# Filling the gaps between dependent VectorE steps in a fused attention and MLP kernel

## The chip, the cores and the metric

The kernel runs on one core of one Trainium2 chip. A core has five engines that run side by side and wait for each other by semaphores: TensorE (PE, matmuls), VectorE (DVE), ScalarE (ACT), GpSimd (POOL) and SyncE (SP, here only a DMA queue). The metric is the device time of one execution in microseconds, the median of three runs. A profile is one execution, recorded instruction by instruction; its span is a little shorter than the time of the run.

## The reference, cut to what matters

Top-k attention over 8 batches, 8 heads, 576 tokens and a head size of 64, and then an MLP with a PReLU whose slope is a vector over the hidden units.

```python
scores = scale * np.matmul(q, k.transpose(0, 1, 3, 2))         # 576 x 576 for each head
kth = np.partition(scores, -top_k, axis=-1)[..., -top_k:-top_k + 1]   # top_k = 32
scores = np.where(scores >= kth, scores, -1000000000.0)
attn = softmax(scores)                                           # written out in the original
x = heads side by side of np.matmul(attn, v)                     # 4608 x 512
h = x @ w_in                                                     # 4608 x 2048
g = np.maximum(h, 0.0) + alpha * np.minimum(h, 0.0)
out = g @ w_out
```

All inputs and the output are fp32. The kernel splits the PReLU as alpha * h + (1 - alpha) * max(h, 0). So the output is x times a precomputed matrix `w_lin` plus max(h, 0) times a scaled `w_out`, and VectorE only has to take the maximum.

## The kernel before: the parts that matter

The work is cut into 144 pieces ("duos"): piece n is two groups of 128 query rows against 576 keys. The main loop is a software pipeline. Turn n of it, called slot n below, handles a different stage of several pieces at once. For one piece the stages are:

1. TensorE forms the scores (`ps_sc`, in PSUM, one buffer). ScalarE copies them to SBUF (`s_sb`).
2. VectorE looks for the 32nd largest score of each row. It takes the top 8 of each of six groups of 96 (MAX8, `up` and `small`), merges them (`bot`, `th`), negates (`neg`) and takes MAX8 again (`n8`). This gives a first threshold `p`.
3. ScalarE compares the row with that threshold (`sg`, a sign) and counts (`cs`). GpSimd multiplies scores and signs (`y`). VectorE takes MAX8 over `y` (two rows of 576), picks the right one by the count (`eq`, `pk`) and sums to the exact threshold `KT`.
4. ScalarE forms `r`, which is huge below the threshold; GpSimd subtracts it from the scores; ScalarE takes Exp (`w`).
5. A DMA transposes `w` to `wT`. TensorE multiplies by v (`xo`). Once in two slots VectorE normalises (`rz`, `x`), and DMA transposes `x` to `xT`.
6. MLP: TensorE forms `ph` = h, VectorE writes max(h, 0) to `gT`, TensorE adds up `pz`, ScalarE copies it out (`o_sb`), and SyncE's DMA stores it. While TensorE has nothing to do, `keep_warm` lets it multiply zeros (`rest`).

Inputs are transposed on TensorE (`tps`) and copied out of PSUM (`qkT`): for each pair of heads two copies of 512 columns and one of 128.

VectorE's part of a slot, with cuts:

```python
norm = on(n - 5) and n % 2 == 0 and n < ND + 4          # every second slot
if on(n):
    for i in range(2):
        for g in range(NG):                             # NG = 6
            m = DVE.max(out=(lo if g % 2 else up)[:, i, g // 2, :], in_=s[:, i, GW * g:GW * g + GW])
            ...
            if i == 0 and g == 1:
                kt_sum(n - 2)                           # KT <- pk
    DVE.tensor_tensor(bot, up, lo[:, :, :, ::-1], ALU.min)
    DVE.tensor_tensor(th[:, :, 0:24] ..., up, lo[:, :, :, ::-1], ALU.max)
    for i in range(2):
        DVE.max(out=th[:, i, 24:32], in_=bot[:, i, :, :])
    if norm:
        norm_a(n - 5)                                   # rz <- xo
else:
    ...
if on(n - 1):
    DVE.tensor_tensor(eq, io9 ..., cs ..., ALU.is_equal)
if on(n):
    DVE.tensor_scalar(neg, th, -1.0, None, ALU.mult)
if on(n - 1):
    DVE.max(out=p9[:, 0, 1:9], in_=y[:, 0, :])          # 576 columns
if norm and on(n):
    norm_b(n - 5)                                       # x <- xo, rz
h_dve()                                                 # gT <- ph
if on(n):
    for i in range(2):
        DVE.max(out=n8[:, i, :], in_=neg[:, i, 0:31])
if on(n - 1):
    DVE.max(out=p9[:, 1, 1:9], in_=y[:, 1, :])
if on(n):
    DVE.tensor_scalar(p9n[:, :, 0:1], n8[:, :, 7:8], -1.0, None, ALU.mult)
...
if on(n - 1):
    DVE.scalar_tensor_tensor(out=pk, in0=eq, scalar=BIG, in1=p9, ...)
```

In slots without normalisation the compiled kernel has `eq` ahead of `bot`, as the instruction list shows.

The main loop, with cuts:

```python
for n in range(ND + 4):                                 # ND = 144
    end = n >= ND
    if not h_pe() and not end:                          # ph, at most one group
        keep_warm()
    ... st_av(m)                                        # xo of piece n - 5
    st_count(n - 1); st_y(n - 1)                        # sg, cs; y
    st_exit(n + 1)                                      # s_sb <- ps_sc
    did = o_pe()                                        # one part of pz, if its PSUM bank is free
    dve_slot(n, late)
    st_relu(n - 2, 0); st_relu(n - 2, 1)                # r; GpSimd's subtraction
    run(n, "prep", ...)                                 # tps
    st_qk(n + 2)                                        # ps_sc
    ... if not (end or ready() > 2) or not o_pe():      # a second part of pz
            if not end and not did:
                keep_warm()
    st_exp(n - 3)                                       # w, wT
    busy = False
    while pend:                                         # copies out of PSUM (qkT)
        tail = n >= 4 and tuple(pend[0][0].shape[2:]) == (64,)
        prep_evac(DVE.tensor_copy if tail else ACT.copy)
        busy = busy or not tail
    run(n, "scale")                                     # w_out scaled: ScalarE and VectorE, 512 columns each
    if end or not busy:
        o_act()                                         # o_sb <- pz
    ...
```

`o_pe` starts no new part while a finished `pz` has not been copied out. After slot 147 a short loop works off what is left of the MLP.

Of the kernel before, what the change touches and what calls it, by code (L numbers as in the profile page):

```python
# [8 lines left out]
FP32 = mybir.dt.float32  # L9
# [8 lines left out]
NG = 6  # L18
# [17 lines left out]
def fast_path(tc, q, k, v, moe_w_in, moe_w_out, moe_alpha, out, flag):  # L36
# [27 lines left out]
    with ExitStack() as ctx:  # L64
# [169 lines left out]
        def dve_slot(n, f_late):  # L234
# [7 lines left out]
            norm = on(n - 5) and n % 2 == 0 and n < ND + 4  # L242
            if on(n):
                s = T["s", n]
                up = two.tile([128, 2, NG // 2, 8], FP32, name="up", tag="up")
                for i in range(2):
                    for g in range(NG):
# [5 lines left out]
                        if i == 0 and g == 1:  # L253
                            kt_sum(n - 2)

# [4 lines left out]
                                     lo[:, :, :, ::-1], ALU.max), [(0, 48)], [(48, 72), (80, 104)])  # L260
                for i in range(2):
                    o = 48 + 32 * i
                    sm(DVE.max(out=th[:, i, 24:32], in_=bot[:, i, :, :]), [f"bot{n % 2}"], [(o + 24, o + 32)])
                if norm:
                    norm_a(n - 5)
            else:
                kt_sum(n - 2)
# [3 lines left out]
            if on(n - 1):  # L271
                y, p9, cs = T.pop(("y", n - 1)), T.pop(("p9", n - 1)), T.pop(("cs", n - 1))
                sm(DVE.tensor_tensor(eq, io9.unsqueeze(1).to_broadcast([128, 2, 9]),
                                     cs.unsqueeze(2).to_broadcast([128, 2, 9]), ALU.is_equal),
                   [(146, 155)], [(128, 146)])
            if on(n):
                neg = two.tile([128, 2, 32], FP32, name="neg", tag="neg")
                sm(DVE.tensor_scalar(neg, th, -1.0, None, ALU.mult), [(48, 112)], [f"neg{n % 2}"])
            if on(n - 1):
                DVE.max(out=p9[:, 0, 1:9], in_=y[:, 0, :])  # L280
            if norm and on(n):
                norm_b(n - 5)
            h_dve()
            if on(n):
                for i in range(2):
                    o = 112 + 8 * i
                    sm(DVE.max(out=n8[:, i, :], in_=neg[:, i, 0:31]), [f"neg{n % 2}"], [(o, o + 8)])
            if on(n - 1):
                DVE.max(out=p9[:, 1, 1:9], in_=y[:, 1, :])
            if on(n):  # L290
                p9n = three.tile([128, 2, 9], FP32, name="p9", tag="p9", bufs=4)
                sm(DVE.tensor_scalar(p9n[:, :, 0:1], n8[:, :, 7:8], -1.0, None, ALU.mult), [(112, 128)], [f"p9{n % 4}"])
# [683 lines left out]
```

The softmax here doesn't subtract the row's maximum and nothing guards it: scores larger than these inputs give would overflow.

## Time and profile before

| what | value |
|---|---|
| time, median of 3 runs | 846.79 us (846.05 to 848.18) |
| span of the profiled execution | 847.1 us |
| TensorE: busy, matmuls recorded | 771.6 us (91%), 5454 |
| granted TensorE clock, mean | 0.976 |
| `y` and the subtraction on GpSimd, 288 each | 362.8 and 363.0 us |
| MAX8 over `y`, 288 on VectorE | 215.3 us, 748 ns each |
| MAX8 over 96 columns, 1728 on VectorE | 428.9 us, 246 to 251 ns each |
| `gT`, 144 on VectorE | 97.6 us, 678 ns each |
| `qkT` of 512 columns, 63 on ScalarE | 35.8 us, 573 ns each |
| `o_sb`, 36 on ScalarE | 20.7 us, 576 ns each |
| `rest` (zeros), 296 matmuls on TensorE | 79.8 us, 400 ns each |

How to read it: an instruction's duration runs from its start to the moment its result is written. The next instruction of the same engine may start before that, so the durations of VectorE add up to more than its busy time, which counts each moment once. What a step costs its engine is the distance from its start to the start of the next one. A row of the timeline gives the start, the duration, the engine, the source line, the operation, what is written from what is read, the shape, and how many instructions are merged in it; a bracket at the end holds the idle time before it and who ended it. Nearly all instructions carry line 31, that of a recording helper, so they are told apart by the names of their tiles.

### The profile page before, as it was taken

Reading aid. Unit: us, or ns where it says so; the run is one execution under the profiler, and the core shown is the slowest. Engines: PE = TensorE matmul, PEld = TensorE weight load, DVE = VectorE, ACT = ScalarE, POOL = GpSimd, SP = SyncE. Lnnn points to the kernel's source line nnn. Section 1 sums busy time; section 2 is a strip of 40 time slices with the busy share of each in tenths; the row PEclk is TensorE's granted clock in tenths of the full one; section 3 lists DMA queues with packets and bytes.
Section 4 is the critical chain, followed back from the end, with each engine's and each line's share of the span. In section 5 each row is a group of like instructions: output and inputs, shape, how many; then the busy total and the mean of one; then the engine's idle time right before and its main releaser. Section 6 shows DMA issues by size and latency. Waiting matters only on the chain.

```text
span 847.1 us, 18646 instructions
## 1 busy us (share of the span) xinstructions
PE 771.6 (91%) x5454; PEld 436.0 (51%) x5454; DVE 784.2 (93%) x3947; ACT 779.3 (92%) x1285; POOL 757.0 (89%) x706
## 2 busy tenths in 40 slices
PE   8778899998999999989999999989989999999886
PEld 5334455555545555555455555555555555555553
DVE  4989999999999999999999999999999999999941
ACT  5999999999999999999999999998999999999840
POOL 3998999999999999999999999998999998999930
PEclk9889999999999999999999999998999999999989
DMA  6899865576657656656466668565565674544441
GB/s 129 187 210 190 163 122 106 89 125 121 124 104 125 124 109 113 126 116 129 102 116 120 119 118 132 110 129 116 91 132 108 119 132 85 95 82 91 84 99 42
DMA packets 344462, 100.29 MB, mean 118 GB/s; under 512 B 338192, under 2 KB 338208, under 8 KB 344352
## 3 DMA queue, kind: packets, MB, share of 16 engines
q1 hardware_dynamic: 341456, 92.42, 58.4%
q0 software_dynamic: 1696, 6.30, 3.1%
q8 instruction: 45, 0.74, 0.4%
q14 instruction: 65, 0.53, 0.2%
q10 hardware_dynamic: 1200, 0.30, 0.2%
HBM read 36.71 MB, written 9.44 MB: 54 GB/s over the span
## 4 chain that ended last, share of the span: by engine, by line
DVE 61%; PE 19%; ACT 14%; issue 2%; DMA 2%; POOL 2%; ACTq 0%; SPq 0%
DVE small L31 17%; DVE p L31 16%; DVE up L31 10%; DVE gT L31 7%; PE pz L31 5%; PE ps_sc L31 5%; ACT sg L31 4%; PE ph L31 4%; ACT s_sb L31 3%; ACT r L31 3%; PE xo L31 3%; DVE neg L31 2%; DVE bot L31 2%; DVE x L31 2%; ACT w L31 2%
## 5 line engine op out<-in xcount | busy, mean ns | idle before, releaser
L31 POOL TENSOR_TENSOR y<-s_sb,sg 128x576 f32<-128x576 f32 x288 | 362.8, 1281 | 55.2 <-ACT sg L31 53.3
L31 POOL TENSOR_TENSOR s_sb<-s_sb,r 128x576 f32<-128x576 f32 x288 | 363.0, 1283 | 0.4 <-ACT r L31 0.2
L31 ACT ACTIVATE sg<-s_sb,p 128x576 bf16<-128x576 f32 x288 | 221.5, 773 | 24.4 <-DVE p L31 23.0
L31 PE MATMUL ps_sc<-qkT 64*128 64x512 f32 (+2 forms) x768 | 184.3, 575 | 45.9 <-ACT s_sb L31 44.9
L31 DVE MAX8 p<-y 128x8 f32<-128x576 f32 x288 | 215.3, 748 | 4.9 <-POOL y L31 4.7
L31 DVE MAX8 up<-s_sb 128x8 f32<-128x96 f32 x864 | 212.3, 246 | 5.3 <-ACT s_sb L31 5.3
L31 DVE MAX8 small<-s_sb 128x8 f32<-128x96 f32 x864 | 216.6, 251 | 0.0
L31 ACT ACTIVATE r<-s_sb,KT 128x576 bf16<-128x576 f32 x288 | 208.5, 776 | 0.8 <-DVE KT L31 0.8
L31 ACT ACTIVATE w<-s_sb 128x1152 bf16<-128x1152 f32 x144 | 166.9, 1159 | 1.0 <-POOL s_sb L31 1.0
L31 ACT COPY s_sb<-ps_sc 128x1152 f32<-128x1152 f32 x144 | 159.1, 1105 | 4.0 <-PE ps_sc L31 4.0
L31 PE MATMUL ph<-xT,w_in_b 128*128 128x256 bf16 (+1 forms) x1408 | 151.4, 255 | 6.1 <-DVE gT L31 3.2
L31 PE MATMUL pz<-w_out_b,gT 128*128 128x512 bf16 x576 | 149.4, 382 | 0.0
L31 PEld LDWEIGHTS <-w_in_b 128*128 128x128 bf16 x1408 | 119.0, 99 | 47.0 <-issue 12.9
L31 PE MATMUL xo<-v,wT 128*128 128x65 bf16 (+3 forms) x1600 | 126.5, 198 | 8.1 <-DMA wT<-w 8.1
L31 PEld LDWEIGHTS <-wT 128*128 128x128 bf16 (+3 forms) x1600 | 97.4, 99 | 42.8 <-DMA wT<-w 10.9
L31 DVE TENSOR_SCALAR gT<-ph 128x512 bf16<-128x512 f32 x144 | 97.6, 678 | 14.8 <-PE ph L31 14.8
L31 PEld LDWEIGHTS ps_sc<-qkT 64*128 64x128 f32 (+1 forms) x768 | 54.0, 170 | 97.6 <-ACT s_sb L31 67.2
L31 PEld LDWEIGHTS ps_sc<-kd,qkT 128*128 128x128 f32 x256 | 39.3, 193 | 100.7 <-issue 99.9
L31 PEld LDWEIGHTS <-gT 128*128 128x128 bf16 x576 | 56.8, 99 | 54.5 <-issue 2.4
L31 PE MATMUL rest<-idle 128*128 128x512 bf16 x296 | 79.8, 400 | 2.9 <-ACT qkT L31 2.1
L31 PE MATMUL ps_sc<-kd,qkT 128*128 128x128 f32 x256 | 64.3, 334 | 0.0
L31 PE MATMUL pz<-w_lin_b,xT 128*128 128x512 bf16 x144 | 56.0, 389 | 0.7 <-ACT o_sb L31 0.7
(56 smaller groups left out, 671.0 us busy)
## 6 DMA issues: line engine op xcount, KB each, us to landing
k_st<-in_k_dram SPq DMA_DIRECT2D x64, 128.0 KB, 2.7
v_st<-in_v_dram SPq DMA_DIRECT2D x64, 128.0 KB, 2.8
out_dram<-o_sb SPq DMA_DIRECT2D x32, 256.0 KB, 2.4
q_st<-in_q_dram SPq DMA_DIRECT2D x62, 128.0 KB, 2.7
w_st<-in_moe_w_out_dram POOLq DMA_DIRECT2D x4, 1024.0 KB, 6.8
wT<-w SPq DMA_TRANSPOSE x144, 3.5
w_in_b<-in_moe_w_in_dram POOLq DMA_DIRECT2D x4, 512.0 KB, 7.2
k_st<-in_k_dram SPq DMA_DIRECT2D x32, 32.0 KB, 2.5
```

What stands on the lines that cost most here:

```text
L31: return self.tc.keep_in_program_order(f(*a, **kw))
```

## The change

It moves steps; no arithmetic is altered. Between two VectorE steps of which the second reads what the first wrote, it places one that depends on neither. In slots without normalisation `kt_sum` follows the last MAX8 over the scores, and the first MAX8 over `y` comes between the MAX8s over `bot` and `neg`. In slots with normalisation the reciprocal comes before `bot`, and the normalisation follows `th`. In the last slots `h_dve` comes first. ScalarE's copy of a finished `pz` goes ahead of Exp, and it is asked for more often. On TensorE `xo` goes ahead of `ph`. Up to slot 16 the 512-column copies of the input transposes go to VectorE and the 128-column ones to ScalarE, later the short ones to VectorE as before; the scalings of `w_out` are spread differently over slots 3 to 14.

```diff
+            def eq_():
+                cs = T.pop(("cs", n - 1))
+                sm(DVE.tensor_tensor(eq, ... ALU.is_equal), ...)
+            def row(i):
+                DVE.max(out=T["p9", n - 1][:, i, 1:9], in_=T["y", n - 1][:, i, :])
             if on(n):
 ...
-                        if i == 0 and g == 1:
+                        if i == (norm == 0) and g == (1 if norm else NG - 1):
                             kt_sum(n - 2)
+                if norm:
+                    norm_a(n - 5)
                 bot = ...
                 sm(DVE.tensor_tensor(bot, up, lo[:, :, :, ::-1], ALU.min), ...)
                 sm(DVE.tensor_tensor(th[:, :, 0:24] ..., ALU.max), ...)
+                if norm:
+                    norm_b(n - 5)
+                elif on(n - 1):
+                    eq_()
                 for i in range(2):
                     sm(DVE.max(out=th[:, i, 24:32], in_=bot[:, i, :, :]), ...)
-                if norm:
-                    norm_a(n - 5)
+                if norm and on(n - 1):
+                    eq_()
+                elif on(n - 1):
+                    row(0)
+                sm(DVE.tensor_scalar(neg, th, -1.0, None, ALU.mult), ...)
+                if norm and on(n - 1):
+                    row(0)
+                h_dve()
+                for i in range(2):
+                    sm(DVE.max(out=n8[:, i, :], in_=neg[:, i, 0:31]), ...)
+                if on(n - 1):
+                    row(1)
+                sm(DVE.tensor_scalar(p9n[:, :, 0:1], n8[:, :, 7:8], -1.0, None, ALU.mult), ...)
             else:
+                h_dve()
                 kt_sum(n - 2)
 ...                                    # the old order of these steps is taken out
         for f in range(NFT):
-            at(3 + f // 2 if f < 8 else f - 1, "scale", lambda f=f: scale_out(f))
+            at((3, 3, 4, 4, 5, 6, 7, 7, 8, 9, 10, 11, 11, 12, 13, 14)[f], "scale", lambda f=f: scale_out(f))
 ...
+            for m in [n - 5, n - 4] if n == ND + 3 else [n - 5]:
+                if on(m):
+                    st_av(m)
             if not h_pe() and not end:
                 keep_warm()
-            for m in [n - 5] if n < ND + 3 else [n - 5, n - 4] if n == ND + 3 else []:
-                if on(m):
-                    st_av(m)
 ...
             if on(n + 2):
                 st_qk(n + 2)
+            if end or ready() > 4 or all(len(d.shape) == 3 for d, _ in pend):
+                o_act()
 ...
-            busy = False
             while pend:
-                tail = n >= 4 and tuple(pend[0][0].shape[2:]) == (64,)
-                prep_evac(DVE.tensor_copy if tail else ACT.copy)
-                busy = busy or not tail
+                short = len(pend[0][0].shape) == 3
+                on_dve = short and n > 16 or pend[0][0].shape[1] == 512 and n < 17
+                prep_evac(DVE.tensor_copy if on_dve else ACT.copy)
 ...
-            if end or not busy:
-                o_act()
```

In the instruction lists of the two kernels the slots without normalisation now read: last MAX8, `KT`, `eq`, `bot`, `th`, two MAX8 over `bot`, MAX8 over `y`, `neg`, `gT`. Those with normalisation read: last MAX8, `rz`, `bot`, `th`, `x`, two MAX8 over `bot`, `eq`, `neg`, MAX8 over `y`, `gT`.

## The prediction

> **What bounds the kernel now.** I read the page first (busy shares, then the chain of work that ended last), next the busy times by window, then VectorE's timeline over two slots, the waits, and TensorE's timeline at the end.
>
> ```profile
> PE 771.6 (91%) x5454; PEld 436.0 (51%) x5454; DVE 784.2 (93%) x3947; ACT 779.3 (92%) x1285; POOL 757.0 (89%) x706
> ...
> DVE 61%; PE 19%; ACT 14%; issue 2%; DMA 2%; POOL 2%; ACTq 0%; SPq 0%
> ```
> Three engines lie within four per cent of each other, but the chain runs through VectorE for 61% of the span: VectorE binds, narrowly.
>
> ```profile
> 400.00:500.00 100.00, 93.62 (x689) 53.36 (x686) 98.83 (x509) 97.88 (x163) 96.05 (x87) 0.98 0.62 116
> ...
> 800.00:820.00 20.00, 15.85 (x161) 11.04 (x160) 11.58 (x39) 11.71 (x20) 12.57 (x11) 0.83 0.56 104
> 820.00:847.00 27.00, 19.98 (x173) 11.85 (x170) 5.45 (x11) 2.13 (x4) 0.00 (x0) 0.94 0.16 47
> ```
> The columns are PE, PEld, DVE, ACT, POOL, then the granted clock. In the middle VectorE is at 98.8% and ScalarE at 97.9%; in the last 47 us only TensorE has much to do, and at 800 to 820 its clock is down to 0.83.
>
> ```profile
> 405.94 0.14 DVE L31 TENSOR_SCALAR p<-small 128x2 f32<-128x2 f32 x1
> ...
> 406.32 0.25 DVE L31 MAX8 small<-s_sb 128x8 f32<-128x96 f32 x1
> 406.48 0.15 DVE L31 TENSOR_REDUCE KT<-pk 128x2 f32<-128x18 f32 x1
> 406.55 0.25 DVE L31 MAX8 up<-s_sb 128x8 f32<-128x96 f32 x1
> ...
> 408.51 0.28 DVE L31 MAX8 small<-bot 128x8 f32<-128x24 f32 x2
> 408.82 0.22 DVE L31 TENSOR_SCALAR neg<-small 128x64 f32<-128x64 f32 x1
> ...
> 411.07 0.14 DVE L31 TENSOR_SCALAR p<-small 128x2 f32<-128x2 f32 x1
> ...
> 416.55 0.14 DVE L31 TENSOR_SCALAR p<-small 128x2 f32<-128x2 f32 x1
> ```
> The two-element p closes each slot, so an odd slot takes 411.07 - 405.94 = 5.13 us and an even one (with the normalisation) 5.48. These two values come back through the whole middle; an even slot with a 128-column qkT copy in it takes 5.70. Durations overlap, so the cost of a step is the distance to the next start: a 0.25 us MAX8 costs 0.16, KT costs 0.07. But neg, which reads what the MAX8 pair wrote, starts 0.31 after it; an independent step starts 0.19 after it. That 0.12 is waiting that the busy share hides.
>
> ```profile
> ACT sg L31 <- DVE p L31: 23.0, 43, 2.2
> DVE gT L31 <- PE ph L31: 14.8, 8, 7.8
> DVE rz L31 <- PE xo L31: 14.4, 13, 2.6
> ```
> ScalarE waits for VectorE's p, little (23 us over 144 slots): it is the next limit. VectorE waits for xo 13 times.
>
> ```profile
> 808.21 1.89 PE L31 MATMUL ph<-xT,w_in_b 128*128 128x128 bf16 x16 [3.20 <-DVE gT L31]
> ```
> At the end TensorE stands 3.2 us for a gT that VectorE has queued behind steps still waiting for their inputs; the 16 matmuls after it take 1.89 us, where the same group takes 1.07 just before.
>
> **What the Trainium skill says.** "VectorE: DVE Perf Modes", The DRAIN you can't avoid, says that a Vector step has a flush behind it and that a step which is not held starts earlier. The trace agrees: 0.16 between independent MAX8s, 0.28 from the last of them to the dependent bot. The same page, Why PSUM operands drop a tier, caps an fp32 source in PSUM at the slowest mode; the trace has 0.69 us on VectorE for the 512-column qkT copy and 0.57 on ScalarE, so moving these copies buys ScalarE time with more of VectorE's. "TensorE: Matmul & The Clock Gate", HAM oscillation, warns that idle gaps bring the clock down. Here it happens after shorter gaps than the page's 3.4 us: after 1.92 us idle at 571.09, the four ps_sc matmuls take 2.08 instead of 1.13. "Perfetto Trace Analysis", Identifying the Most-Contended Engine, takes occupancy as a fair measure for Vector; here part of it is the 0.12 waits.
>
> **The change part by part.**
>
> Odd slots on VectorE. KT moves behind the last MAX8, into the 0.28 before bot. KT (0.16 after that MAX8), eq (+0.07) and bot (+0.07) make 0.30 where the trace has 0.29, so KT's 0.07 elsewhere is freed and 0.01 paid. A 576-column p goes between the bot MAX8s and neg, which frees the 0.12. Sum 0.18: 5.14 becomes 4.96.
>
> Even slots. The reciprocal (0.08) moves into the 0.28 before bot: free. But between the bot MAX8s and neg only eq is left, so neg waits 0.19 + 0.12 instead of 0.19 + 0.08 + 0.06. Gain 0.02: 5.48 becomes 5.46. Moving x (0.32) only changes its place.
>
> Four slots of the middle on VectorE (two odd, two even, one 128-column copy of 0.20 to 0.22): 5.14 + 5.70 + 5.14 + 5.48 = 21.46 before, 4.96 + 5.68 + 4.96 + 5.46 = 21.06 after, 1.9% less.
>
> ScalarE over the same four: sg, sg, s_sb copy, two r and w start 0.77, 0.76, 1.00, 1.34 and 1.05 us apart, 4.92 in all, and each 512-column copy (qkT or o_sb) adds 0.47. Three in four slots: 4 x 4.92 + 3 x 0.47 = 21.09. The change moves o_sb ahead of Exp but removes nothing here, so ScalarE stops VectorE's gain at about 21.1: the two become level. GpSimd's y starts are 5.29, 5.39, 5.23 and 4.94 apart when it doesn't wait, 20.85: just below. Three engines level within one per cent do not interlock without loss; I take 5.30 us a slot instead of 21.06 / 4 = 5.27.
>
> Slots 24 to 123 take 543.0 us now (150.8 to 693.8): 5.43 each, of which 536.5 is 25 x 21.46 and the rest xo waits and slots with two gT. After: 5.30, plus 0.02 for waits of that kind, is 532. Gain 11.
>
> Waits for xo. Attention's matmuls now come before h. An h group takes 0.87 us to the next start, but the reciprocal asks 0.56 earlier (0.16 after the last MAX8 instead of 0.28 + 0.12 + 0.12 + 0.19 = 0.71, rounded in the trace), so the margin grows by only 0.3. The x20 slots, with waits of 0.7, keep about half. Twenty groups of idle matmuls disappear (160 instructions fewer on TensorE, eight to a group) because o_pe finds its PSUM bank free more often. I count about 17 slots in which nothing fills TensorE between xo, h and the next scores, against six before: more gaps of 1.7 to 1.9 us, more slow-clock stretches. With h out of the way most cost some 0.2 us, so I set the net to zero.
>
> First 17 slots (to 111.6 us). ScalarE is at 29.8 of 30 us from 30 to 60. Ten 512-column copies leave it (4.7 us) and three short ones come (0.6); VectorE takes ten of 0.60 (6.0). Slots 3 to 16 on ScalarE: 14 x 4.92 + 16 scalings of 0.62 + small copies = 80; VectorE comes to 78; today's 84.7 contains a stop, near 60 us, in which xo and tps waited on loads and which cost ScalarE 2.6 us; the change does not touch it. 84.7 - 82.6 is 2.1, and 0.4 more from the copies in slots 0 to 2: gain 2.5. Slots 17 to 23: 1.
>
> Slots 124 to 143: ScalarE has few copies left, so VectorE's 0.10 a slot comes through: 2, and 0.5 from xo.
>
> The end. gT first removes the 3.2 us stop and most of the slow stretch (808 to 813: ph 0.8, xo 0.3, pz 1.0 over their usual times, about 2.1). Two output parts fewer remain behind slot 144 (14 instead of 16, at 1.08 each): 2.2. Sum 7.5. Against it, KT comes one gT (0.6) later and so do the last Exp and its transposes; those end before TensorE reaches them. I take 6.
>
> Sum: 11 + 0 + 2.5 + 1 + 2.5 + 6 = 23. From 846.8 this gives 824. Each term assumes that nothing new waits; I leave 2 us for that and predict 826.
>
> **The rivals.** (1) ScalarE becomes the bound earlier than I say, or GpSimd does. For: 97.9% and 96.1% busy. Then the middle stays at 5.36 to 5.40 a slot, the gain there is 3 to 7 and the time is 830 to 838. (2) TensorE's clock falls more often, as idle matmuls are gone. For: the gap at 571 cost VectorE 1.87 us; against: in only three of about six such gaps before did xo come late. If each of 17 gaps costs 1 us, the time is 838 to 842. (3) o_sb ahead of Exp waits on pz and stops ScalarE. Usually the part is done 1.4 us before; after a slow stretch not. A wait of 0.5 us in ten slots is 5 us: 831. (4) ScalarE absorbs more than I think because its short slots fall well, and the end gains the full 7.5: 819.
>
> **Range and chances.** Two per cent is 829.9. My 826 lies 4 us below that, while rivals 1 and 3 cross it. Range 817 to 837. Faster by over 2%: 0.68; within 2%: 0.29; slower: 0.03, as nothing in the change adds work to the binding engine after slot 17.
>
> **What would show it.** Odd slots of 4.96 and even slots of 5.46 where VectorE leads; an average near 5.3; ScalarE's wait for p well below 23 us in the middle, VectorE's waits for y and cs (ScalarE's counts) above; DVE no busier than before. No 3.2 us stop at the end, and less than 38 us from the last p to the end of the span, against 42.8 now. Wrong if odd slots stay above 5.1, if PEclk falls below 0.95, or if ScalarE shows waits for pz in the middle.

## The result and the profile after

The changed kernel takes 838.23 us (median of 4 runs, 837.63 to 838.66) where the kernel before takes 846.59 (4 runs on the same chip, 846.05 to 848.18). The ratio is 0.9898, 95% interval 0.9881 to 0.9915: 1% faster. The prediction was 826, or 2.4% faster. The two profiled spans are 847.1 and 836.9 us, 10.2 apart; the prediction's terms added up to 23. I cut both spans at VectorE's two-element `p`, which closes a slot:

| stage | before | after | gain | predicted |
|---|---|---|---|---|
| to the end of slot 16 | 111.57 | 110.58 | 1.0 | 2.5 |
| slots 17 to 23 | 39.20 | 38.26 | 0.9 | 1 |
| slots 24 to 123 | 543.04 | 538.54 | 4.5 | 11 |
| slots 124 to 143 | 110.50 | 107.63 | 2.9 | 2.5 |
| from the last `p` to the end of the span | 42.79 | 41.89 | 0.9 | 6 |

Two terms fell, the middle and the end; the early one came to less than half. First the page of the changed kernel, busy shares and the engines' shares of the chain of work that ended last:

```profile
PE 744.9 (89%) x5289; PEld 425.0 (51%) x5374; DVE 780.2 (93%) x3954; ACT 774.5 (93%) x1278; POOL 755.2 (90%) x706
...
DVE 49%; PE 23%; ACT 15%; DMA 6%; issue 3%; POOL 1%; SPq 1%; ACTq 0%
```

VectorE's share of the chain falls from 61% to 49%, while TensorE and DMA rise to 23% and 6%. VectorE has stopped leading in parts of the span, and other engines' waits have come in. Next, busy times by window of the changed kernel (length, then PE, PEld, DVE, ACT, POOL, granted clock, DMA share, GB/s):

```profile
400.00:500.00 100.00, 90.36 (x665) 52.21 (x677) 98.05 (x504) 97.96 (x162) 96.22 (x89) 1.00 0.61 120
...
812.00:837.00 25.00, 16.18 (x150) 10.29 (x152) 5.45 (x11) 1.76 (x3) 0.00 (x0) 0.90 0.13 41
```

In the middle VectorE (98.05%) and ScalarE (97.96%) are level, as predicted. At the end TensorE is busy for 16.18 of 25 us: the end still contains stops. VectorE's timeline of the changed kernel over an even and an odd slot:

```profile
406.43 0.14 DVE L31 TENSOR_SCALAR p<-small 128x2 f32<-128x2 f32 x1
...
408.48 0.25 DVE L31 MAX8 small<-s_sb 128x8 f32<-128x96 f32 x1
408.64 0.16 DVE L31 RECIPROCAL rz<-xo 128x4 f32<-128x4 f32 x1
408.76 0.20 DVE L31 TENSOR_TENSOR bot<-up,small 128x48 f32<-128x48 f32 x1
...
411.88 0.14 DVE L31 TENSOR_SCALAR p<-small 128x2 f32<-128x2 f32 x1
...
414.40 0.28 DVE L31 MAX8 small<-bot 128x8 f32<-128x24 f32 x2
414.64 0.76 DVE L31 MAX8 p<-y 128x8 f32<-128x576 f32 x1
415.32 0.21 DVE L31 TENSOR_SCALAR neg<-small 128x64 f32<-128x64 f32 x1
...
416.90 0.14 DVE L31 TENSOR_SCALAR p<-small 128x2 f32<-128x2 f32 x1
```

The even slot takes 411.88 - 406.43 = 5.45 us (predicted 5.46), the odd one 416.90 - 411.88 = 5.02 (predicted 4.96; 4.93 to 4.94 occurs too). The fillers do what they are for: `rz` sits inside the 0.28 us between the last MAX8 and `bot`, and the row of `y` has removed the wait ahead of `neg`. Yet slots 24 to 123 take 5.39 us on average. The time goes at the places where something waits, so to the waits of the changed kernel (us in total, times, longest):

```profile
PE xo L31 <- DMA wT<-w: 22.7, 18, 5.8
ACT o_sb L31 <- PE pz L31: 22.0, 6, 7.6
...
ACT sg L31 <- DVE p L31: 12.1, 24, 1.2
```

ScalarE's wait for `p` has halved from 23.0, as a faster VectorE should make it. The line to notice is `xo` waiting for `wT`: 22.7 us, against 8.1 before. And in slots 24 to 123 ScalarE's `o_sb` waits for `pz` three times (1.9 us), where it never did before. That was one of the things named as showing the prediction wrong.

### The profile page after: what moved, and what is told of

Read it like the earlier page. It is cut to its first block, busy times and chain, and to the rows that moved or that the text cites. A ratio compares the mean times of both kernels' runs of the same rounds, so it can differ in the third digit from the quotient of the medians.

```text
span 836.9 us, 18387 instructions
## 1 busy us (share of the span) xinstructions
PE 744.9 (89%) x5289; PEld 425.0 (51%) x5374; DVE 780.2 (93%) x3954; ACT 774.5 (93%) x1278; POOL 755.2 (90%) x706
## 4 chain that ended last, share of the span: by engine, by line
DVE 49%; PE 23%; ACT 15%; DMA 6%; issue 3%; POOL 1%; SPq 1%; ACTq 0%
DVE small L31 15%; DVE p L31 13%; DVE up L31 8%; PE ps_sc L31 7%; PE pz L31 6%; DVE gT L31 6%; DMA wT<-w 4%; ACT sg L31 4%; PE xo L31 4%; ACT r L31 4%; PE ph L31 4%; ACT s_sb L31 3%; ACT w L31 2%; DVE x L31 1%; DVE neg L31 1%
## 5 line engine op out<-in xcount | busy, mean ns | idle before, releaser
L31 PE MATMUL xo<-v,wT 128*128 128x65 bf16 (+3 forms) x1600 | 127.3, 199 | 24.4 <-DMA wT<-w 22.7
L31 PE MATMUL pz<-w_out_b,gT 128*128 128x512 bf16 x554 | 144.5, 382 | 3.5 <-DVE pk L31 0.2
L31 PEld LDWEIGHTS <-w_in_b 128*128 128x128 bf16 x1408 | 109.0, 98 | 15.5 <-issue 0.2
L31 PE MATMUL rest<-idle 128*128 128x512 bf16 x198 | 57.9, 401 | 2.5 <-DVE qkT L31 0.9
L31 ACT ACTIVATION_READ_ACCUMULATOR sg<-s_sb,p 128x1 f32 x288 | 55.7, 193 | 0.0
```

Source lines behind the costliest of these rows:

```text
L31: return self.tc.keep_in_program_order(f(*a, **kw))
```

## The experiments

Each ratio is to the kernel before on the same chip, with its 95% interval. Executions of one kernel can differ by up to 9.1 us (849.12 to 858.23 in the first case below), so a stage value, which comes from one profile, is relied on only where several kernels agree or the difference is far larger.

**VectorE's order alone.** All else as before: `h_pe` ahead of `st_av`, `o_act` behind Exp, old copies, old last slots. Against the changed kernel:

```diff
+            if not h_pe() and not end:
+                keep_warm()
             for m in [n - 5, n - 4] if n == ND + 3 else [n - 5]:
                 if on(m):
                     st_av(m)
-            if not h_pe() and not end:
-                keep_warm()
 ...   # o_act, copies and last slots: as undone one by one below
```

> VectorE's new order alone; output copies, first transposes, order of xo and h and the last slots as before. Theory A (the freed VectorE time is real, but the reciprocal now asks for xo 0.56 us earlier while TensorE still does h first): undisturbed odd slots near 5.0 us and even ones at 5.46, VectorE's waits for xo up from 14.4 us to 22 or more, time 839 to 843. Theory B (the order frees nothing, ScalarE takes it; the 8 us of the change come from its other parts): four slots stay at 21.4, time 845 to 847.

Measured: 854.11 us, 1.0085 (1.0045 to 1.0124). The reordering that gives the change its point is a loss by itself. The profiled execution is the quickest of the six; its span, 847.3, is that of the kernel before (847.1), so it does not show where the slower ones lose. Their times follow the granted clock: 849.12 to 851.83 us at 0.982 to 0.985, 856.39 to 858.23 us at 0.972 to 0.975. What the profile shows is that nothing is gained: odd slots take 4.94, and the middle still takes 544.46 us. From its waits:

```profile
DVE rz L31 <- PE xo L31: 29.6, 35, 2.6
```

`rz` waited for `xo` 14.4 us in the kernel before and waits 29.6 here; in slots 24 to 123 alone it is 22 waits and 14.1 us instead of 5 and 4.5. One of them, from the timelines of VectorE and TensorE of this kernel:

```profile
402.47 0.18 DVE L31 RECIPROCAL rz<-xo 128x4 f32<-128x4 f32 x1 [0.52 <-PE xo L31]
```
```profile
400.79 1.03 PE L31 MATMUL ph<-xT,w_in_b 128*128 128x256 bf16 x8
401.66 0.78 PE L31 MATMUL xo<-v,wT 128*128 128x65 bf16 x10
```

The h group starts at 400.79 and holds `xo` back by 0.87, until 401.66; the reciprocal, now asked for earlier, stops for 0.52. What the fillers freed on VectorE is spent waiting for `xo`.

**Attention ahead of h alone**, in the kernel before:

```diff
+            for m in [n - 5] if n < ND + 3 else [n - 5, n - 4] if n == ND + 3 else []:
+                if on(m):
+                    st_av(m)
             if not h_pe() and not end:
                 keep_warm()
-            for m in ... (the same three lines)
```

> The kernel before, with only xo moved ahead of h on TensorE. Theory A (order of VectorE and order of TensorE are worth something only together): waits for xo in the middle (4.5 us) go, odd and even slots stay at 5.14 and 5.48: 841 to 844. Theory B (xo first is the gain by itself, VectorE's order nothing): 835 to 838.

Measured: 838.53 us, 0.9884 (0.9857 to 0.991). One moved loop gives as much as the whole change. The middle takes 540.2 us, with odd slots still at 5.14 and no wait of `rz` for `xo` in it. Stage by stage it is 3.4, 0.8, 2.8, 1.5 and 1.8 us shorter than the kernel before, so most of the gain lies outside the middle. Over the whole span:

```profile
PE xo L31 <- DMA wT<-w: 14.9, 13, 2.3
...
DVE rz L31 <- PE xo L31: 5.1, 4, 2.6
```

The waits for `wT` show up here already: they come with attention's place at the head of TensorE's slot.

**The whole change without it.** In the changed kernel only the two blocks of the first diff are exchanged.

> The changed kernel with h ahead of xo on TensorE again. Theory A (xo first is what makes the earlier reciprocal affordable): waits for xo rise from 11.9 to 20 us or more, time 842 to 846. Theory B (xo first does harm, as TensorE now stands for wT with h behind it: waits for wT were 10.9 us before and 31.3 after on the weight loads): waits for wT back near 11 us, gT waits for ph down from 19.3, time 834 to 837.

Measured: 848.10 us, 1.0014 (0.9997 to 1.0031). Without attention ahead of h the other four parts together give nothing; the middle even takes 546.3 us, with 14.4 us of waits of `rz` for `xo`. The fillers give VectorE time that only an earlier `xo` lets it use; how much that is then worth is shown further down.

**The output copy behind Exp again.** In the changed kernel:

```diff
-            if end or ready() > 4 or all(len(d.shape) == 3 for d, _ in pend):
-                o_act()
 ...
+            busy = False
             while pend:
 ...
+                busy = busy or not short
 ...
+            if end or not busy:
+                o_act()
```

> The changed kernel with the output copies behind Exp and only in slots without a 512-column copy, as before. Theory A (freeing the bank of pz earlier packs two output parts into slots in which TensorE is already full, which costs the 8 us of late slots in the middle): slots 51, 52, 87, 88 and 119 to 122 come back to 5.0 to 5.7 us, the middle (slots 24 to 123) takes 532 to 534 us instead of 538.5, while four more parts wait at the end (2 to 4 us there): time 834 to 838. Theory B (the earlier copies are a gain): time 841 to 844.

Measured: 835.38 us, 0.9858 (0.9826 to 0.9889). The middle takes 532.84 us, 5.7 less than in the changed kernel and what the prediction had for it. Slots 124 to 143 take 1.7 us more (109.30), as the second output parts come later (16 of them, instead of 14, are left behind the last `p`). The same edit was made in two other variants below, where the middle went from 538.49 to 534.41 and from 538.42 to 532.64. In three pairs of profiles, then, what was done to the copy costs the middle 4 to 6 us. With the first transposes as before the difference is smaller: 540.91 with the copy ahead of Exp, 536.77 and 538.39 with it behind (below). It gives some back later (1.4 to 1.7 in slots 124 to 143 and up to 1.6 at the end), so putting it back is worth 2.9, 2.1 and -0.3 us of the time. It can cost in three ways: by its place in ScalarE's queue; by freeing `pz` earlier, so that TensorE packs its parts differently; or, being asked for more often, by falling into slots that have a 512-column copy already. The next two runs, read slot by slot, tell the first two apart.

**The place, with the old packing.** The copy is ahead of Exp, but behind the second `o_pe`, so that TensorE's list of instructions is that of the run just shown:

```diff
-            if end or ready() > 4 or all(len(d.shape) == 3 for d, _ in pend):
-                o_act()
 ...   # behind the second o_pe:
+            if end or all(len(d.shape) == 3 for d, _ in pend):
+                o_act()
             if on(n - 3):
                 st_exp(n - 3)
```

> The changed kernel with the output copy still ahead of Exp, but asked for only after the second output part and only in slots without a 512-column copy, so TensorE's list is that of the run with the copy behind Exp, step for step. Theory A (the packing of parts on TensorE is what costs): 834.5 to 836.5, middle 532 to 534 us. Theory B (the place ahead of Exp is what costs, as Exp and the transposes behind it come later or the copy waits for pz): 838 to 840, middle 537 to 539 us.

Measured: 847.98 us, 1.0005 (0.9992 to 1.0018). With TensorE's work the same, one place in ScalarE's queue costs 12.6 us, more than either theory had; in the profiles it is 4.4 in the middle (537.28) and 7.2 at the end (49.04). In the middle nearly all of it lies in slots 61 to 63 (2.2) and 97 to 99 (1.9). Slot 61 shows how, first TensorE, then ScalarE, GpSimd and VectorE:

```profile
350.23 0.79 PE L31 MATMUL xo<-v,wT 128*128 128x65 bf16 x10 [1.73 <-DMA wT<-w]
350.96 1.59 PE L31 MATMUL ph<-xT,w_in_b 128*128 128x256 bf16 x8
...
352.77 1.91 PE L31 MATMUL pz<-w_out_b,gT 128*128 128x512 bf16 x4
```
```profile
354.72 0.58 ACT L31 COPY o_sb<-pz 128x512 f32<-128x512 f32 x1 [2.16 <-PE pz L31]
```
```profile
357.20 2.52 POOL L31 TENSOR_TENSOR y<-s_sb,sg 128x576 f32<-128x576 f32 x2 [2.34 <-ACT sg L31]
```
```profile
352.59 0.69 DVE L31 TENSOR_SCALAR gT<-ph 128x512 bf16<-128x512 f32 x1 [0.86 <-PE ph L31]
...
355.01 0.29 DVE L31 COPY qkT<-tps 128x128 f32<-128x128 f32 x1 [0.67 <-PE tps L31]
```

Read them in order. `wT` is late and TensorE stands for 1.73 us. After that its matmuls run slowly: eight of h take 1.59 instead of 1.05, the output part 1.91 instead of 1.03. The part is done 2.16 us after ScalarE asked for it, and ScalarE, which could have run Exp, stands in front of it. Exp, the next signs and then GpSimd's products are late by as much. VectorE stops too, but for the slow matmuls themselves: 0.86 us for `gT` and 0.67 for `tps`. With the copy behind Exp TensorE had waited only 1.34 us in this slot, its matmuls were not slow, and the copy did not wait (TensorE of the run before this one):

```profile
348.69 0.79 PE L31 MATMUL xo<-v,wT 128*128 128x65 bf16 x10 [1.34 <-DMA wT<-w]
...
350.51 1.03 PE L31 MATMUL pz<-w_out_b,gT 128*128 128x512 bf16 x4
```

The longer wait comes from the place, three slots earlier. There the copy puts Exp back by 0.47 us; SyncE's queue, full of transposes and loads, hands that on, and the `wT` of slot 61 is issued 0.46 us later, both counted from the `p` that closes slot 60. At the end of this kernel ScalarE's stop is far longer. ScalarE, then TensorE:

```profile
809.98 0.59 ACT L31 COPY o_sb<-pz 128x512 f32<-128x512 f32 x1 [5.06 <-PE pz L31]
```
```profile
815.09 0.91 PE L31 MATMUL xo<-v,wT 128*128 128x65 bf16 x10 [4.53 <-DMA wT<-w]
```

The copy waits 5.06 us for its part, Exp starts behind it, and TensorE then stands 4.53 us for the `wT` that comes from that Exp. So the place alone can cost much. But it is not what the changed kernel lost in the middle: there slots 61 to 63 and 97 to 99 take as long as with the copy behind Exp, within 0.1 us each, while the slots in which it does lose are untouched here.

**One output part in slots with much h.** In the changed kernel the second part is held back where the slot already had 16 matmuls of h:

```diff
+            heavy = not end and bool(act and act[-1][2] == 4)
             late = ...
 ...
-                if not (end or ready() > 2) or not o_pe():
+                if heavy and did or not (end or ready() > 2) or not o_pe():
```

> The changed kernel, with at most one output part in a slot whose h group has 16 matmuls. Theory A (packing): the waits in slots 51, 52, 87, 88 and 119 to 122 go, 4 to 6 us of the middle, and three more parts at the end cost 1 to 3: 834 to 837. Theory B (place of the copy): 838 to 841.

Measured: 841.42 us, 0.9911 (0.9879 to 0.9942). The end takes 4.1 us more (45.94), since what is not done in the middle is left for it. The middle is only 1.9 us shorter (536.61), but its slots say more than the sum. Slots 52, 88, 122 and 123 together take 24.9 us in the changed kernel (24.9 to 25.1 in the other three of this section that differ from it only in their first or last slots), 21.9 here, and 21.9 to 22.0 in both runs above. Slot 52 of the changed kernel, VectorE and TensorE, and then the same of this one:

```profile
299.02 0.14 DVE L31 TENSOR_SCALAR p<-small 128x2 f32<-128x2 f32 x1
...
302.80 0.18 DVE L31 RECIPROCAL rz<-xo 128x4 f32<-128x4 f32 x1 [1.26 <-PE xo L31]
```
```profile
301.12 1.03 PE L31 MATMUL pz<-w_out_b,gT 128*128 128x512 bf16 x4
301.98 0.78 PE L31 MATMUL xo<-v,wT 128*128 128x65 bf16 x10
```
```profile
301.76 0.14 DVE L31 TENSOR_SCALAR p<-small 128x2 f32<-128x2 f32 x1
```
```profile
302.25 0.79 PE L31 MATMUL xo<-v,wT 128*128 128x65 bf16 x10 [0.16 <-DMA wT<-w]
```

In the changed kernel a second output part stands ahead of attention, which starts 2.96 us after the `p` that closes slot 51, and `rz` waits 1.26 us for it. Without that part attention starts after 0.49 us, and `rz` does not wait. The packing is thus worth 3.0 of the 5.7 us, with the copy's place unchanged.

Slots 51, 79, 80, 83 and 87 are 2.0 us longer in both kernels than with the copy behind Exp. In four of them VectorE waits for ScalarE's counts (0.34 us in slot 51), soon after a slot in which ScalarE made both an `o_sb` and a 512-column `qkT` copy (49, 78, 85). The two runs above have neither such slots nor such waits, so this belongs to the copy's being asked for more often; no run changes that alone. The remaining differences, 2.6 us more in slots 115 to 121 and 1.0 less in each of slots 58 and 94, are not taken apart here. That this run's middle gains no more than 1.9 us comes from slots 34, 44 and 55, which are 3.0 us longer in it than in the changed kernel.

**KT first in the last slots.** In the changed kernel:

```diff
             else:
-                h_dve()
                 kt_sum(n - 2)
+                h_dve()
 ...
-            if f_late:
+            if f_late and on(n):
                 h_pe()
                 h_dve()
 ...   # behind pk:
+            if f_late and not on(n):
+                h_pe()
+                h_dve()
```

> The changed kernel, but in the last slots KT goes ahead of gT and pk ahead of the late gT. Theory A (in the changed kernel KT stands behind a gT that waits for ph, so r, the output copy behind r and TensorE behind that copy all come 2 us late): from the last p to the end of the span 39 to 40 us instead of 41.9, time 835.5 to 836.8. Theory B (the end is set by TensorE's remaining work and the last store): no change, 838.

Measured: 837.12 us, 0.9881 (0.9845 to 0.9916); the end takes 39.62 us instead of 41.89.

**The old order in the last slots**, otherwise the changed kernel:

```diff
             else:
-                h_dve()
                 kt_sum(n - 2)
 ...
                     row(0)
+                h_dve()
+                if on(n - 1):
                     row(1)
```

> The changed kernel with the kernel before's order in the last slots: key sums and normalisation ahead of gT. If h first in the last slots is what gives the end anything, the end (last p to end of span) goes from 41.9 us to 44 or more and the time to 840 or more. If it gives nothing because KT then stands behind a gT that waits for its matmuls, the end stays at 40 to 42 us and the time at 836 to 838.5.

Measured: 836.21 us (835.99 to 836.67), 0.9873 (0.9851 to 0.9896); the end takes 40.06. h first in the last slots, which was to give most of the 6 us, costs about 2. The changed kernel's end, first VectorE, then ScalarE, then TensorE:

```profile
801.83 0.69 DVE L31 TENSOR_SCALAR gT<-ph 128x512 bf16<-128x512 f32 x1 [1.64 <-PE ph L31]
802.43 0.16 DVE L31 TENSOR_REDUCE KT<-pk 128x2 f32<-128x18 f32 x1
```
```profile
802.69 1.44 ACT L31 ACTIVATE r<-s_sb,KT 128x576 bf16<-128x576 f32 x2 [2.94 <-DVE KT L31]
804.04 0.56 ACT L31 COPY o_sb<-pz 128x512 f32<-128x512 f32 x1
```
```profile
804.65 0.38 PE L31 MATMUL pz<-w_lin_b,xT 128*128 128x512 bf16 x1 [1.97 <-ACT o_sb L31]
```

A loop of four engines: `gT` waits 1.64 for its matmuls; the 0.16 us of `KT` stands behind it; ScalarE's `r` waits 2.94 for `KT`; the output copy stands behind `r`; TensorE waits 1.97 for the copy. With the old order `KT` ran before that `gT`, and TensorE's part started without a wait (VectorE and TensorE):

```profile
799.75 0.17 DVE L31 TENSOR_REDUCE KT<-pk 128x2 f32<-128x18 f32 x1
801.22 0.69 DVE L31 TENSOR_SCALAR gT<-ph 128x512 bf16<-128x512 f32 x1 [1.29 <-PE ph L31]
```
```profile
801.98 0.38 PE L31 MATMUL pz<-w_lin_b,xT 128*128 128x512 bf16 x1
```

**First transposes as before.** In the changed kernel:

```diff
-            at((3, 3, 4, 4, 5, 6, 7, 7, 8, 9, 10, 11, 11, 12, 13, 14)[f], "scale", ...)
+            at(3 + f // 2 if f < 8 else f - 1, "scale", ...)
 ...
-                on_dve = short and n > 16 or pend[0][0].shape[1] == 512 and n < 17
+                on_dve = short and n >= 4
```

> The changed kernel with the first transposes' copies given back to ScalarE and the scalings spread as before. Theory P (VectorE's ten copies only move the load, as both engines meet the same stop on loads near 60 us): within 1 us of the changed kernel's 838, slots 0 to 16 at 109 to 111 us. Theory Q (my prediction's 2.5 us): 840 to 842, slots 0 to 16 at 112.5 to 113.5 us.

Measured: 836.18 us (833.25 to 838.76), 0.9861 (0.9828 to 0.9894). The stage to slot 16 gets shorter by 2.4 us (108.17) instead of longer. In the changed kernel slots 0 to 7 take 54.5 us instead of 56.2, so the copies' move does free ScalarE there; but slots 8 to 11 take 27.0 instead of 23.2. There TensorE and VectorE of the changed kernel meet this:

```profile
54.43 1.07 PE L31 MATMUL xo<-v,wT 128*128 128x65 bf16 x10 [5.81 <-DMA wT<-w]
```
```profile
61.96 0.18 DVE L31 RECIPROCAL rz<-xo 128x4 f32<-128x4 f32 x1 [3.99 <-PE xo L31]
```

With the old copies the longest wait for `wT` up to slot 9 is 1.15 us and that of `rz` 1.18. The late `wT` of the changed kernel is under way from 46.77 to 54.39, beside a load of 512 KB of `w_in_b` that is issued at 47.48 and lands at 54.98. With the old copies that load is issued 2.3 us behind the transpose, and the transpose lands after 4.1 us instead of 7.6. That the load holds it up is likely, but no run moves the load. The early gain of the old copies was not kept in this profile: its middle took 540.91. Over the three pairs of kernels that differ by these copies alone the old ones give -2.0 us (here), 0.0 and +2.7 (below), so the move is worth nothing that can be named.

**VectorE's order and attention ahead of h, nothing else.** Undone are the output copy, the first transposes and the last slots:

```diff
 # the diffs of "the output copy behind Exp again", "first transposes as before"
 # and "the old order in the last slots", together
```

> VectorE's new order and attention ahead of h, alone; output copies, first transposes and last slots are those of the kernel before. Theory P (these two parts are the whole gain, the other three give nothing or take away): at least as fast as the kernel with only the output copy put back (0.986 of before), 831 to 836 us; slots 24 to 123 at 532 to 535 us, slots 0 to 16 at 108 to 110, the end at 41 to 42.5. Theory Q (moving the first transposes off ScalarE is worth the 2.5 us that I gave it, and h first in the last slots helps too): slower than that kernel by 2 to 5 us, 837 to 841; slots 0 to 16 at 111.5 or more.

Measured: 836.49 us, 0.9874 (0.985 to 0.9899), with stages of 108.68, 38.25, 536.77, 109.09 and 42.11. These two parts give all that the whole change gives. But attention ahead of h alone came to 0.9884, so VectorE's new order adds 0.1%, less than the intervals can tell. It does show in the middle, which is 3.4 us shorter than with attention ahead of h alone, and 1.8 to 7.6 us shorter in the five kernels of this section that have this middle with the copy behind Exp and nothing else changed in it. The time is half a microsecond above what theory P had, as the middle is longer than its 532 to 535; theory Q's 111.5 us to slot 16 are not there.

**The three I would keep**: the same, but with `KT` first in the last slots.

```diff
 # the diffs of "the output copy behind Exp again", "first transposes as before"
 # and "KT first in the last slots", together
```

> VectorE's new order, attention ahead of h, and last slots with KT ahead of gT; the output copy and the first transposes as before. Theory P: the fastest of all, 830 to 834 us (0.980 to 0.985 of before): middle 532 to 535, slots 0 to 16 at 108 to 110, end 40 to 41.5. Theory Q (first transposes on VectorE are worth 2.5): 836 to 838.

Measured: 837.76 us, 0.9893 (0.9867 to 0.9919); middle 538.39. It is not the fastest, and where its time agrees with theory Q the reason does not: the stage to slot 16 takes 107.74 us, less than in the changed kernel. The same with the changed kernel's first transposes:

```diff
 # the diffs of "the output copy behind Exp again" and "KT first in the last slots", together
```

> The changed kernel with the output copies as before and with KT ahead of gT and pk ahead of the late gT in the last slots. Theory A (the two faults are independent): middle 533, from the last p to the end 39 to 40.5 us: 832.5 to 834. Theory B (with four more parts at the end TensorE sets the end anyway): 835, as without it.

Measured: 835.03 us, 0.9847 (0.9823 to 0.9871), as in theory B; middle 534.41. Between these two, which have the same code from slot 17 on, the middle differs by 4 us. Most of it sits in slots 43 to 46 and 115 to 116, where `xo` waits for `wT` in both (1.92 and 1.38 us in the quicker kernel, 1.83 and 2.02 in the slower). What differs is the pace behind the wait. Slot 43 on TensorE, first of the slower kernel, then of the quicker:

```profile
250.78 0.79 PE L31 MATMUL xo<-v,wT 128*128 128x65 bf16 x10 [1.83 <-DMA wT<-w]
251.50 2.90 PE L31 MATMUL ph<-xT,w_in_b 128*128 128x256 bf16 x16
```
```profile
252.16 0.79 PE L31 MATMUL xo<-v,wT 128*128 128x65 bf16 x10 [1.92 <-DMA wT<-w]
252.88 1.92 PE L31 MATMUL ph<-xT,w_in_b 128*128 128x256 bf16 x16
```

After 1.83 us idle the same 16 matmuls take 2.90 us, after 1.92 us they take 1.92. In slot 115 the slower kernel's output part takes 1.91 instead of 1.03. So the two middles differ by where TensorE happened to run slowly, and differences of this size between single profiles carry that chance with them.

The wait for `wT` itself recurs every 18 slots: 43, 61, 79, 97, 115. In SyncE's own queue of the changed kernel stand four transposes of the remainder tile, then loads, then `wT`:

```profile
241.87 4.99 SPq L31 DMA_TRANSPOSE xT<-xm  x4
...
248.84 1.39 SPq L31 DMA_TRANSPOSE wT<-w  x1
```

**Those four spread over two slots**, with the output copy behind Exp:

```diff
             if on(n - 5) and n % 2 == 0 and n < ND + 4:
                 st_xT(n - 6)
-                st_xT(n - 5)
+                if duos[n - 5][0] == "n":
+                    st_xT(n - 5)
+            elif on(n - 6) and duos[n - 6][0] != "n":
+                st_xT(n - 6)
```

> The kernel with the output copy put back behind Exp, and in addition the four transposes of the remainder tile (xT from xm) issued two in one slot and two in the next, instead of four in a row on SyncE's queue. Theory A (every 18 slots xo waits for wT because those four hold SyncE's queue for 5 us, and h behind it pays): TensorE's waits for wT in slots 24 to 123 fall from 7.1 us to under 3, no slot of 43, 61, 79, 97 and 115 shows more than 0.5; the middle goes from 532.8 to 530 to 531.5, the time from 835.4 to 832 to 834. Theory B (wT is late for another cause, or the wait is hidden): waits or time stay, 835 to 836.

Measured: 835.05 us, 0.9846 (0.9819 to 0.9874). In slots 24 to 123 TensorE's wait for `wT` falls from 7.1 to 2.1 us and is gone from all five slots, so the cause was right. The middle takes 533.47, no less than 532.84. Slot 43, first SyncE's queue, then TensorE:

```profile
241.19 2.44 SPq L31 DMA_TRANSPOSE xT<-xm  x2
...
245.61 1.38 SPq L31 DMA_TRANSPOSE wT<-w  x1
```
```profile
249.64 0.78 PE L31 MATMUL xo<-v,wT 128*128 128x65 bf16 x10
250.35 1.92 PE L31 MATMUL ph<-xT,w_in_b 128*128 128x256 bf16 x16
```

`wT` is issued at 245.61 and attention starts at 249.64 without waiting. Slot 43 takes 5.01 us instead of 5.69, and slot 116 is 0.26 shorter. In slots 61, 79 and 97 the waits were slack: these slots and the next ones take the same as before, within 0.1 us. The 0.9 us gained are lost again in slots 66, 74 and 110, which are 1.9 us longer here; TensorE's matmuls run slowly just before, after idle times of 1.98, 1.75 and 1.66 us.

**h ahead of attention in every 18th slot**, with the output copy behind Exp:

```diff
+            if n % 18 == 7:
+                h_pe()
             for m in [n - 5, n - 4] if n == ND + 3 else [n - 5]:
                 if on(m):
                     st_av(m)
-            if not h_pe() and not end:
+            if n % 18 != 7 and not h_pe() and not end:
                 keep_warm()
```

> The kernel with the output copy put back, but in every 18th slot (7, 25, 43, 61, and so on) h goes ahead of attention again, as in the kernel before. Theory A (attention ahead of h costs something just where wT is late): TensorE's wait for wT in these slots shrinks by the length of an h group (0.9 us), gT's waits for ph go, and the time falls by up to 1.5 us, 833.5 to 835. Theory B (h ahead only delays xo there, whose wT then is there): xo waits of 0.5 us and more in the slot behind, the time is 835.5 to 837.

Measured: 834.49 us, 0.9838 (0.9808 to 0.9868); the wait for `wT` in the middle is 2.8 us, that of `gT` for `ph` zero, the middle 532.34. Again slots 43 and 116 gain 0.9 us together, and slots 74 and 110 lose 0.7. The time lies in theory A's range, but 0.9 us below the kernel without this edit is within the spread of executions.

**The output copy behind Exp and the old last slots:**

```diff
 # the diffs of "the output copy behind Exp again" and "the old order in the last slots", together
```

> The changed kernel without two of its parts: the output copy is behind Exp again, and the last slots have their old order; VectorE's order, attention ahead of h and the first transposes stay. If the two losses add up (2.9 and 2.0 us when undone alone), 832.5 to 834; if the old order at the end gains only where the output copy is ahead of Exp, 835 to 836, with an end of 41 to 42 us.

Measured: 836.48 us (833.74 to 838.78), 0.9877 (0.9847 to 0.9908). The two gains do not add up: behind Exp the copy no longer closes the loop through `KT` (the longest wait of a matmul for `o_sb` at the end is 0.72 us with either order), and the end takes 41.19 us, against 41.85 with h first. **With the transposes spread as well:**

```diff
 # the diffs of "the output copy behind Exp again", "the old order in the last slots"
 # and "those four spread over two slots", together
```

> The one before with the transposes of the remainder tile spread over two slots as well. Theory A: the fastest of all, 830.5 to 833. Theory B: as the one without the spread, within 1 us.

Measured: 834.51 us, 0.9844 (0.9817 to 0.9872), not the fastest by any margin. The versions at 834.5 to 835.4 us take 1.4 to 1.6% less than the kernel before and cannot be told apart; their lead over the changed kernel's 0.9898 (0.9881 to 0.9915) is at the edge of what the intervals tell. The simplest of them is the changed kernel with the output copy behind Exp.

## Why the prediction was wrong, step by step

- **VectorE's slots: right.** 5.45 predicted as 5.46; 4.94 to 5.02 predicted as 4.96. The two MAX8 over `bot` cost 0.24 to the next start where I took 0.19, which is most of the rest.
- **"Waits for xo ... net to zero": right for the sum of two effects, and I did not see their size.** The order alone raises the waits of `rz` in the middle from 4.5 to 14.1 us; attention ahead of h alone takes them to none and is worth the whole gain of the change. Together, with the output copy behind Exp, 2.3 us are left and the middle takes 532.84 us in that profile, against 532 predicted (532.64 to 538.39 in the five kernels with this middle). Outside the middle attention ahead of h is worth 7.5 us by itself, 3.4 of them in the first 17 slots, for which I had counted 0.5. A margin of 0.3 us stood for two opposite shifts of 0.56 and 0.87, each of which moved the total by several us.
- **"The change moves o_sb ahead of Exp but removes nothing here": the step that failed in the middle.** I priced what happens to the copy at zero in the sum and kept its waits for `pz` as the third rival, at 5 us. The size came, 5.7 us when this part alone is undone, but by another mechanism, so that the rival's number is luck: the copy waits for `pz` three times in the middle, 1.9 us in all. 3.0 us come from packing. I had seen that `o_pe` finds its PSUM bank free more often and counted only the idle matmuls that this saves, not that a second output part then stands ahead of attention. 2.0 us more lie behind slots in which ScalarE has two large copies. The place ahead of Exp costs 4.4 us in the middle when it is tried with the old packing, in other slots than these.
- **"The end. gT first removes the 3.2 us stop ... I take 6": failed.** The stop went, and a new one came by way of `KT`, `r` and the output copy. I had seen that `KT` would come one `gT` later and took that as harmless, since I counted the 0.6 us of the step and not the 1.64 us it would itself wait. The parts left behind the last `p` did fall, from 16 to 14, as I had it. From the last `p` to the start of the last output copy it is 33.5 us instead of 36.6: 3.1 gained. From there to the end of the span it is 8.35 instead of 6.17: 2.2 lost, behind all the work (see below).
- **First 17 slots, 2.5: failed.** I left today's stop near 60 us out of the sum as untouched. It is not: with ScalarE relieved, slots 0 to 7 are 1.7 us shorter than with the old copies, and slots 8 to 11 are 3.8 longer, with waits for `wT` of 5.81 and for `xo` of 3.99.
- **Slots 17 to 23 and 124 to 143: right** (0.9 and 2.9 for 1 and 2.5).
- **Rivals 1 and 2.** ScalarE is level with VectorE, but with the copy behind Exp and nothing else changed the middle comes to 5.33 a slot, so that level is not what cost the 6.5 us. The clock did not fall in the profile, 0.979 against 0.976 (0.970 to 0.975 in the other three executions), with `rest` down from 296 to 216 matmuls by its weight loads; the trace has 198 of them.
- **Two loose readings.** That "in the last 47 us only TensorE has much to do" holds from 820 us on; from 800 to 820 VectorE, ScalarE and GpSimd are busy for 11.6 to 12.6 of the 20 us. And the 1.92 us idle at 571.09 was followed by slow matmuls, but 1.93 us idle at 376.67 and at 616.00 in the same kernel was not (1.13 us for the four `ps_sc` matmuls both times).

In sum: of the 12.8 us between the 23 of my terms and the 10.2 of the two profiles, 6.5 lie in the middle, 5.1 at the end, 1.5 in the first 17 slots, and the two stages that went right give 0.3 back.

What stays open: the 2.2 us behind the last output copy. It is 8.1 to 8.7 us from that copy to the end in all seven kernels with the copy ahead of Exp and 6.1 to 6.4 in the eleven others. In the seven, two of SyncE's closing semaphore instructions, which run after the last store has landed, start 2.0 to 2.3 us apart (4.31 and 2.16 us before the end in the changed kernel); in the others the same ones start 0.1 us apart. So no engine's work is late there, but why SyncE stands is not shown. Nor did any run show why TensorE runs slowly after one idle time and not after another of the same length.

## What to carry to other kernels

Freeing time on the engine that leads pays only if its inputs come earlier too: look for the step that will now ask sooner, and move its producer ahead in its own queue first. A copy that waits for another engine should not stand ahead of work that is ready in an in-order queue, above all on an engine as busy as the leader; and moving a step behind another also moves it behind whatever that one waits for. Freeing a buffer sooner also lets its producer run sooner, and in an in-order queue that can put its work ahead of what the leading engine needs next. A wait in the profile is worth removing only if what follows was late because of it: two experiments here removed 4 to 5 us of waits, and the slots that had them became 0.9 us shorter. And a cause is better looked for slot by slot than in the sum of a stage, where it mixes with unrelated gains and losses.

## What the runs showed that I had not expected

An idle TensorE of 1.73 us can be followed by slow matmuls: 1.59 us for eight of h instead of 1.05, and 1.91 for four of the output part instead of 1.03. It need not be: after 2.11 us idle in slot 43 of the kernel with the copy behind Exp, 16 of h take their usual 1.92. The Trainium skill ("TensorE: Matmul & The Clock Gate", HAM oscillation) names a longer gap, about 3.4 us; the measurement decides, as it did in the kernel before. On SyncE's queue four transposes in a row take 4.99 us, about 1.25 each, so they put off whatever is behind them by almost a slot. And four executions of the same kernel on the same chip spread over 5.5 us in one case and 1 us in others.
